# Three parts of a fused attention and feed-forward kernel redone: the value product of the first blocks, the decoding of weights, and the order of the work

## The chip, the cores and the metric

One core of a Trainium2 chip runs the whole program. Its engines are PE (TensorE, matrix products into PSUM), DVE (VectorE), ACT (ScalarE), POOL (GpSimd) and SP (SyncE, which here issues all the transfers from and to HBM and the transposes that the DMA engines make). [...] The metric is the time of the program on the device in microseconds, as the median of several runs; one execution was also taken by the profiler.

## The reference, cut to what matters

Three layers follow each other on 2304 tokens of width 512: attention with 8 heads in a window of 128 tokens, a feed-forward layer with a softmax gate and a layer norm (512 to 1024 to 512), and one with a sigmoid gate (512 to 2048 to 512).

```python
def _attn_ref(q, k, v):                      # 4 batches, 8 heads, 576 tokens, 64
    scores = scale * np.matmul(q, k.transpose(0, 1, 3, 2))
    scores = np.where(mask, scores + bias[None], -1000000000.0)
    scores = scores - np.max(scores, axis=-1, keepdims=True)
    attn = np.exp(scores)
    attn = attn / (np.sum(attn, axis=-1, keepdims=True) + 1e-09)
    return np.matmul(attn, v)
def _moe_ref(x, w_in, w_out, g_ln):
    h = x @ w_in
    sm = np.exp(h - h_max) / (sum + 1e-09)
    solu = h * sm
    ln = (solu - mu) / np.sqrt(var + 1e-06) * g_ln
    return ln @ w_out
def _moe2_ref(x, w_in, w_out):
    h = x @ w_in
    return (h * (1.0 / (1.0 + np.exp(-h)))) @ w_out
```

The weights arrive as float64, the rest as float32. The kernel's large products are made in pairs of float16 parts (high times high, high times low, low times high), three matmuls for each product.

## The kernel before, in words

The tokens are cut into 18 blocks of 128. For each block the kernel does attention (`a_qk`, `a_max` and what follows), the first feed-forward layer (`m1_in`, `layer_norm`), and for each pair of blocks, a chunk of 256 tokens, `m1_out` and then the second layer in eight steps (`m2_in`, `m2_out`).

**Weights.** Four matrices fill 48 slots of 512 float32 columns of one large tile `W`: w_in in slots 0 to 7, w_out in 8 to 15, w2_in in 16 to 31, w2_out in 32 to 47. `load_weight` (L452) takes two slots at a time: two loads of 512 KB into one `stage` buffer, of which there are two (`N_STAGE`). `decode` (L421) makes float32 of the two words of each float64: ACT works on the high words (L435), DVE casts the low words (L437) and puts the two together (L439), each over 1024 columns, both slots at once. Then the squares of each slot are summed for a scale (L473 to L489), and `split_weight` (L498) makes the two float16 parts. In `split_weight` a letter of `E_W` and of `PICK` gives each slot's operations to DVE, ACT or POOL.

**Attention of the first four blocks** (`ON_PE["a"]` is T). `a_qk` (L637) makes the scores in the bank pair `SA`, and `a_max` (L659) takes each query's maximum on DVE (L674). `t_parts` (L718) cuts the maxima into three bfloat16 parts (L729 to L732, on POOL in blocks 1 to 3) and turns them on PE (L735, copied at L738). `t_scores` (L742) makes the scores a second time, with keys on the partitions (L759, L765), and subtracts the maxima by a product (L781), so that ACT's exponents (L788) already stand as the value product needs them. `t_av` (L791) then has the values as stationary operand (128 keys x 64) and the exponents as moving one (128 keys x 128 queries); the result stands feature by feature, heads j = 0 and 1 in the two halves of the partitions. The sum of the exponents is made with a block of ones as stationary operand (L809), after a small constant is put there (L806), so that every feature's row holds the same sums.

```python
T.matmul(SA[j * HALF:(j + 1) * HALF, 0, at:at + P], vr[sl][:, 2 * p + j, :],
         a[:, j, c * P:(c + 1) * P], start=(c == 0), stop=(c == nh - 1))
...
T.matmul(SA[j * HALF:(j + 1) * HALF, 1, at:at + P], ones32.tile, a[:, j, c * P:(c + 1) * P],
         start=False, stop=(c == nh - 1))
```

`t_evac` (L813) takes for each half of the heads the reciprocal of 256 columns of sums (L824), multiplies (L827), and writes the two float16 parts (L340, L353) directly into `xT`, the turned operand of `m1_in`. A float32 product is two records in the profile.

**Attention of the other blocks.** The exponents stand query by query, are cut into float16 parts, turned by a DMA transpose (L714) and multiplied with split values (L851). `a_evac` (L856) divides, and x is then turned either on PE (`turned_parts`, L543, with the transposes of L552 and one copy and one subtraction of 512 columns, L554 and L555) or by a DMA transpose that SP issues (L879), as `ON_PE["x"]` says. The letters of that for blocks 0 to 3 are D, D, P, P, and before the change they are not used, since `t_evac` does the turning.

**The order.** Every operation is given to a list planner (`Sched`). An operation's priority is `RANK[kind] + SLOPE[kind] * i` plus an entry of `LATER` for its block; `solve` (L181) plays the engines through with modelled durations and emits each engine's instructions in the order in which they started in that model. Each engine, and SP's queue of transfers too, then works through its own list strictly in order. Pools (`Pool`) hold buffers; one with `after=` opens when the named one is closed.

Of the kernel before, what the change touches and what calls it, by code (L numbers as in the profile page):

```python
# [17 lines left out]
P = 128  # L18
# [37 lines left out]
class Op:  # L56
    __slots__ = ("turn", "buf", "alts", "eng", "cost", "fn", "prio", "succ", "n_dep", "ready", "start", "end", "idx", "dma", "done")

    def __init__(self, alts, prio, idx, dma=0):
# [9 lines left out]
        ("G", "G"): 100}  # L69


class Sched:
# [108 lines left out]
    def solve(self):  # L181
# [4 lines left out]
        todo = [o for o in self.ops if o.n_dep == 0]  # L186

# [28 lines left out]
        while n_left:  # L216
# [37 lines left out]
            t = max(free[o.eng], o.ready, port if held else 0)  # L254
            o.done, o.start = True, t
# [43 lines left out]
def fused_kernel(ctx, tc, qk, qn, kn, vt, rel, w_in, w_out, g_ln, w2_in, w2_out, out):  # L299
# [6 lines left out]
    early = Pool("early", side="right")  # L306

# [3 lines left out]
    pools = [const, early, ps, ps_early, ps_late]  # L311
# [17 lines left out]
    def act(n, fn, r=(), w=(), extra=0):  # L329
        s.op([("A", ca(n, extra), fn, False)], r, w)  # L330
# [46 lines left out]
    ones32 = Buf(early, [P, HALF], F32, "ones32")  # L377
    small = Buf(early, [P, P], BF16, "small")
# [42 lines left out]
    def decode(st, slots, at):  # L421

        def flat(x):
            return x.rearrange("p a c -> p (a c)")

        def out():
            return W.tile.bitcast(U32)[:, slots[0]:slots[1] + 1:slots[1] - slots[0], :]

        def high():
            return st[:, :, :, 1]  # L430
        w = [(W, sl) for sl in slots]
        both = [(st, 0), (st, 1)]
        if DECODE[at // 2] == "A":

            act(1024, lambda: A.activation(flat(high().bitcast(F32)), flat(high().bitcast(F32)), AF.Prelu,  # L435
                                           scale=2.0 ** 16, alpha=-2.0 ** 32), both, [(st, "high")])
            v(1024, lambda: V.tensor_scalar(flat(st[:, :, :, 0]), flat(st[:, :, :, 0]), 2.0 ** -29, 7.0, ALU.mult,  # L437
                                            ALU.min), both, [(st, "low")], fast=True)
            v(1050, lambda: V.scalar_tensor_tensor(out=out(), in0=high(), scalar=3, in1=st[:, :, :, 0],  # L439
                                                   op0=ALU.logical_shift_left, op1=ALU.bitwise_or),  # L440
              [(st, "low"), (st, "high")], w)
            return
        v(1050, lambda: V.tensor_scalar(out(), high(), 3, 0x3FFFFFFF, ALU.logical_shift_left,
                                        ALU.bitwise_and), both, w)
        v(1050, lambda: V.scalar_tensor_tensor(out=out(), in0=high(), scalar=0xC0000000, in1=out(),
                                               op0=ALU.bitwise_and, op1=ALU.bitwise_or), both + w, w)
        v(1050, lambda: V.scalar_tensor_tensor(out=out(), in0=st[:, :, :, 0], scalar=29, in1=out(),
                                               op0=ALU.logical_shift_right, op1=ALU.bitwise_or), both + w, w)
# [3 lines left out]
    def load_weight(name, w, slot0, n, cols, gain=None, columns=False, by_rows=False):  # L452
# [263 lines left out]
    x16, xT, mxs, turned_max, sts = {}, {}, {}, {}, {}  # L716

    def t_parts(i):  # L718
# [8 lines left out]
        def small_op(fn, r, w):  # L727
            s.op([("V", 85, lambda: fn(V), False), ("G", 200, lambda: fn(G), False)], r, w, pick=("tp", i))
# [62 lines left out]
    def t_av(i, p):  # L791
# [19 lines left out]
        pe(300 + 430 * nh, go, [a, ones, ones32, small] + list(vr.values()), [(SA, ("x", p % 2)), (SA, ("x", 2 + p % 2))])  # L811

    def t_evac(i, g):  # L813

        s.at("tevac", i, 10 * g)
        if g == 0:
            xT[i] = Buf(const, [P, 2, KD, P], F16, "xT", N_XT)
        t = xT[i]
        xm = Buf(const, [P, 2, 2, P], F32, "xm", 1)
        x, r = (lambda: xm[:, 0]), (lambda: xm[:, 1])  # L820

        def area(j):
            return SA[:, j, 2 * P:].rearrange("p (a t) -> p a t", t=P)
        v(256, lambda: V.reciprocal(r(), area(1)), [(SA, ("x", 2)), (SA, ("x", 3))], [(xm, 1)])  # L824
        b, z = i * P // S, (i * P + P - 1) // S
        for n, (y, lo, hi) in enumerate([(b, 0, P)] if b == z else [(b, 0, HALF), (z, HALF, P)]):
            v(2 * (hi - lo), lambda y=y, lo=lo, hi=hi: V.scalar_tensor_tensor(  # L827
                out=x()[:, :, lo:hi], in0=area(0)[:, :, lo:hi], scalar=v_scale[y].tile, in1=r()[:, :, lo:hi],
                op0=ALU.mult, op1=ALU.mult), [(SA, ("x", 0)), (SA, ("x", 1)), (xm, 1), v_scale[y]], [(xm, (0, lo))])
        xs = [(xm, (0, lo)) for lo in ((0,) if b == z else (0, HALF))]  # L830
        copy(("xh", i), 256, lambda: t[:, 0, 2 * g:2 * g + 2, :], x, xs, [(t, (0, g))])
        combine(("xl", i), 256, ALU.subtract, lambda: t[:, 1, 2 * g:2 * g + 2, :], x,
                lambda: t[:, 0, 2 * g:2 * g + 2, :], xs + [(t, (0, g))], [(t, (1, g))])
# [22 lines left out]
    def a_evac(i):  # L856
# [10 lines left out]
          [(SA, ("x", p)) for p in range(4)] + [r], [xm])  # L867
        if ON_PE["x"][i] == "P":
# [144 lines left out]
    def m2_in(c, j):  # L1013
# [16 lines left out]
        g = gp[c, j] = Buf(const, [P, 2, 2, TB], F16, "g", N_G)  # L1030
# [41 lines left out]
    s.op([("G", 250, lambda: G.memset(ones32.tile, 1.0), False)], [], [ones32])  # L1072
    s.op([("G", 350, lambda: G.memset(mparts.tile, 0.0), False)], [], [mparts])
    s.op([("G", 250, lambda: G.memset(small.tile, 0.0), False)], [], [small])
    eps = []
    for row in (0, 32, 64):
        rest = np.float32(1e-9) - np.float32(sum(eps))
        eps.append(np.float32(np.uint32(np.float32(rest).view(np.uint32) & 0xFFFF0000).view(np.float32)))
        s.op([("G", 150, lambda row=row, val=float(eps[-1]): G.memset(small[row:row + 1, :], val), False)], [], [small])
# [56 lines left out]
    for c in range(NB // 2 + 1):  # L1136
# [20 lines left out]
RANK = {"aturn": 7557.0, "av": 1601.5, "evac": -1523.1, "exp": 4766.2, "gate": -1551.3, "in": -1067.1, "in2": -263.2,  # L1157
        "load": -3596.7, "lparts": -774.7, "max": 93.3, "max1": 527.0, "norm": -7739.4, "out": -1862.5,
        "out2": 1886.9, "parts": -1408.5, "qk": 1366.1, "s0": 81.8, "s16": 807.4, "s32": 459.9, "s8": 3154.1,
        "share": -670.5, "store": 2132.5, "table": -5031.6, "tav": 99.9, "tevac": 376.2, "texp": 668.6,  # L1160
        "tpar": 2261.5, "tscore": -107.3, "tsub": 382.3, "vload": 815.2, "vnorm": -753.3, "vsplit": 444.8,
        "w0": 1558.8, "w16": 8.5, "w32": 987.0, "w8": -39.6, "xturn": -1082.2, "y": 120.5}
SLOPE = {"aturn": 55.5, "av": -16.8, "evac": 7.64, "exp": 19.41, "gate": -4.84, "in": 30.11, "in2": 1.55,
# [152 lines left out]
```

## Time and profile before

| | |
|---|---|
| median of 3 runs | 764.21 us (764.07 to 764.75) |
| the profiled execution | 760.28 us, its span 758.5 us |
| mean granted clock of PE | 0.962 |
| matmul records on PE | 5670, busy 703.5 us |

The span runs from the first to the last instruction. The profiled execution's own time is 1.8 us longer than its span, and the median of the runs is 3.9 us above the profiled execution. Busy time of PE is modelled and overlaps, so it doesn't say how close PE is to its peak. "Idle before" is the time that the engine stood still just before an instruction, and the arrow names what ended it.

### The profile page before, as it was taken

What the parts mean: (1) busy time and instruction counts of PE and PEld (TensorE: products, weight loads), DVE (VectorE), ACT (ScalarE), POOL (GpSimd) and SP (SyncE); (2) the same over time, 40 slices, a digit from 0 to 9 for tenths busy, and PEclk for the clock granted to TensorE, in tenths of its full rate; (3) what the DMA queues carried; (4) which work ended last, traced back from release to release, by engine and by line L of the source; (5) the groups of instructions that cost most, each with busy time, mean ns of one, the idle gap of its engine ahead of it and who ended that gap; (6) DMA issues with size and microseconds to landing.
All of it is one profiled execution on the core that took longest, in us unless ns stands there. A gap on an engine that the chain in (4) does not pass through costs nothing.

```text
span 758.5 us, 14323 instructions
## 1 busy us (share of the span) xinstructions
PE 703.5 (93%) x5670; PEld 478.3 (63%) x5670; DVE 458.2 (60%) x1204; ACT 357.7 (47%) x735; POOL 130.4 (17%) x126
## 2 busy tenths in 40 slices
PE   4576678999999999999999999999999999999998
PEld 3452444777765557867665777775547668757853
DVE  2569998799795685744457466466895472222220
ACT  4247665799563443644444446354562242222231
POOL 1113415342331021010021302032201010100000
PEclk9785788899999999999999999999999999999999
DMA  9265664179502475444073455154651400400000
GB/s 317 96 208 199 236 191 153 32 187 264 117 30 46 83 150 98 99 111 80 18 166 72 85 102 135 44 129 65 115 117 22 84 15 23 49 28 2 1 29 28
DMA packets 128131, 76.37 MB, mean 101 GB/s; under 512 B 110016, under 2 KB 110656, under 8 KB 128064
## 3 DMA queue, kind: packets, MB, share of 16 engines
q1 hardware_dynamic: 128064, 75.46, 41.0%
q8 instruction: 44, 0.72, 0.4%
q14 instruction: 23, 0.19, 0.1%
HBM read 44.24 MB, written 4.72 MB: 65 GB/s over the span
## 4 chain that ended last, share of the span: by engine, by line
PE 79%; DVE 11%; ACT 5%; DMA 2%; issue 2%; POOL 0%; SPq 0%; DVEq 0%; ACTq 0%; POOLq 0%
PE mm L1052 23%; PE mm L1025 22%; PE mm L893 11%; PE mm L988 11%; PE sa L647 6%; PE sa L851 2%; DVE W L439 2%; DVE xm L824 2%; DMA aT<-a 1%; PE st L765 1%; PE sa L803 1%; DVE sa L674 1%; DVE stage L437 1%; PE sa L809 1%; ACT stage L435 1%
## 5 line engine op out<-in xcount | busy, mean ns | idle before, releaser
L1025 PE MATMUL mm<-y,W 128*128 128x256 f16 x1728 | 207.0, 273 | 1.1 <-DVE t L1035 0.7
L1052 PE MATMUL mm<-W,g 128*128 128x512 f16 x864 | 205.3, 379 | 0.0
L1025 PEld LDWEIGHTS <-W 128*128 128x128 f16 x1728 | 166.6, 98 | 38.4 <-issue 1.4
L1052 PEld LDWEIGHTS <-g 128*128 128x128 f16 x864 | 81.3, 98 | 79.4 <-issue 0.6
L893 PE MATMUL mm<-W,xT 128*128 128x512 f16 x432 | 105.4, 392 | 4.7 <-POOL W L353 3.3
L988 PE MATMUL mm<-lnT,W 128*128 128x256 f16 x864 | 102.7, 273 | 0.7 <-DMA lnT<-ln 0.3
L988 PEld LDWEIGHTS <-W 128*128 128x128 f16 x864 | 83.8, 98 | 18.5 <-issue 1.8
L1034 ACT ACTIVATE t<-mm,cs 128x512 f32<-128x512 f32 x72 | 48.1, 680 | 82.7 <-PE mm L1025 82.7
L1038 DVE SCALAR_TENSOR_TENSOR g<-t,g 128x512 f16<-128x512 f32 x72 | 53.1, 741 | 52.9 <-ACT g L1037 52.5
L1035 DVE SCALAR_TENSOR_TENSOR t<-t,mm 128x512 f32<-128x512 f32 x72 | 48.8, 682 | 52.9 <-ACT t L1034 52.7
L687 ACT ACTIVATE e<-e,mx 128x256 f32<-128x256 f32 (+1 forms) x112 | 55.0, 492 | 50.1 <-DVE mx L682 49.8
L353 POOL TENSOR_TENSOR a<-e,a 128x512 f16<-128x512 f32 (+1 forms) x32 | 39.1, 1221 | 227.5 <-ACT a L340 116.9
L893 PEld LDWEIGHTS <-xT 128*128 128x128 f16 x432 | 43.0, 100 | 55.4 <-issue 13.3
L647 PE MATMUL sa<-k,q 64*128 64x128 f32 x544 | 55.5, 322 | 22.1 <-DVE mxs L674 10.6
L1037 ACT ACTIVATE g<-t 128x512 f16<-128x512 f32 x72 | 44.7, 625 | 64.8 <-PE mm L1052 59.0
L647 PEld LDWEIGHTS sa<-k,q 64*128 64x128 f32 x544 | 40.6, 204 | 42.9 <-DVE mxs L674 15.1
L907 DVE TENSOR_REDUCE lnst<-mm 128x1 f32<-128x1024 f32 x18 | 22.0, 1223 | 49.9 <-PE mm L893 47.1
L682 DVE CUSTOM_DVE_ANT_0 e<-sa,table 128x256 f32<-128x256 f32 (+1 forms) x112 | 43.7, 408 | 14.0 <-PE sa L647 4.8
L909 ACT ACTIVATE e<-mm,lnst,sig 128x1024 f32<-128x1024 f32 x18 | 21.5, 1197 | 38.8 <-DVE lnst L908 18.8
L353 POOL TENSOR_TENSOR W<-W 128x512 f16<-128x512 f32 x19 | 26.3, 1392 | 45.5 <-ACT W L340 26.0
L353 POOL TENSOR_TENSOR ln<-e,ln 128x1024 f16<-128x1024 f32 x9 | 20.6, 2293 | 77.7 <-DVE ln L341 38.9
L993 ACT ACTIVATE y<-mm,cs 128x512 f16<-128x512 f32 x18 | 12.1, 684 | 46.0 <-PE mm L988 34.6
(177 smaller groups left out, 791.9 us busy)
## 6 DMA issues: line engine op xcount, KB each, us to landing
stage<-in_moe_w_in_dram SPq DMA_DIRECT2D x24, 512.0 KB, 4.7
stage<-in_moe_w_out_dram SPq DMA_DIRECT2D x24, 512.0 KB, 4.6
k<-in_kn_dram SPq DMA_DIRECT2D x18, 256.0 KB, 3.0
q<-in_qn_dram SPq DMA_DIRECT2D x18, 256.0 KB, 3.2
vraw<-in_vt_dram SPq DMA_DIRECT2D x18, 256.0 KB, 3.0
out_dram<-t SPq DMA_DIRECT2D x18, 256.0 KB, 2.0
t<-in_vt_dram SPq DMA_DIRECT2D x16, 256.0 KB, 4.4
aT<-a SPq DMA_TRANSPOSE x56, 3.1
```

The source lines that it names most:

```text
L353: ("G", cg(n), lambda: G.tensor_tensor(dst(), a(), b(), op), True)], r, w, pick=pick)
L647: T.matmul(SA[:, j, sl * P:(sl + 1) * P], q[rows, p, :], k[rows, p, :], start=True, stop=sl not in blank)
L682: v(n + 20, lambda j=j: V.tensor_tensor_reduce(e[:, j, lo:lo + n], SA[:, j, lo:lo + n], table[:, 2 * p + j, o:o + n], -0.125, 3.0e38, ALU. ...
L687: act(n, lambda j=j: A.activation(e[:, j, lo:lo + n], e[:, j, lo:lo + n], AF.Exp, bias=mx[:, j:j + 1], scale=-1.0, accum_out=rs[:, 2 * p + ...
L893: T.matmul(pt[:, half * 512:(half + 1) * 512], x[:, hx, k, :], W16(2 * k + half, hw), start=(k == 0 and hx + hw == 0), stop=(k == KD - 1 a ...
L988: T.matmul(pt[:, ct % 2], W16(8 + k, hw)[:, ct * P:(ct + 1) * P], l[:, hx * KF1 + k, :], start=(k == 0 and hw + hx == 0), stop=(k == KF1 - ...
L1025: T.matmul(pt[:, mm], W16(16 + 4 * k + m // 4, hw)[:, (m % 4) * P:(m % 4 + 1) * P], y[:, hx, k, :], start=(k == 0 and hw + hx == 0), stop= ...
L1034: act(512, lambda: A.activation(t.tile, flat(pt.tile), AF.Tanh, scale=cs[:, 0:1]), [pt, (cs, 0)], [t], extra=1)
L1035: v(512, lambda: V.scalar_tensor_tensor(out=t.tile, in0=t.tile, scalar=1.0, in1=flat(pt.tile), op0=ALU.add, op1=ALU.mult), [t, pt], [t])
L1037: act(512, lambda: A.activation(flat(g[:, 0]), t.tile, AF.Copy, scale=2.0 ** -16), [t], [(g, 0)])
L1038: v(512, lambda: V.scalar_tensor_tensor(out=flat(g[:, 1]), in0=t.tile, scalar=2.0 ** -16, in1=flat(g[:, 0]), op0=ALU.mult, op1=ALU.subtrac ...
L1052: T.matmul(pt.tile, g[:, hg, mm, b * P:(b + 1) * P], W16(32 + m, hw), start=(m == 0 and hg + hw == 0), stop=(m == KF2 - 1 and hg == 1))
```

## The change

**The value product of the first four blocks.** The exponents become the stationary operand and the values the moving one, with a 65th column of ones beside the 64 of each head. So the result comes query by query, and its 65th column is the sum. `ones32`, `small` and the fills of POOL for them go; `v_load` now loads into rows of 65 and POOL writes ones into the 65th column for the blocks whose values are needed so.

```diff
-        at = 2 * P + (p % 2) * P
...
-            for c, (sl, _) in enumerate(halves):
-                for j in range(2):
-                    T.matmul(SA[j * HALF:(j + 1) * HALF, 0, at:at + P], vr[sl][:, 2 * p + j, :],
-                             a[:, j, c * P:(c + 1) * P], start=(c == 0), stop=(c == nh - 1))
             for j in range(2):
-                T.matmul(SA[j * HALF:(j + 1) * HALF, 1, at:at + P], ones[:, :HALF], small.tile, start=True, stop=False)
-            for c in range(nh):
-                for j in range(2):
-                    T.matmul(SA[j * HALF:(j + 1) * HALF, 1, at:at + P], ones32.tile, a[:, j, c * P:(c + 1) * P],
-                             start=False, stop=(c == nh - 1))
+                for c, (sl, _) in enumerate(halves):
+                    at = 2 * P + j * (D + 1)
+                    T.matmul(SA[:, p % 2, at:at + D + 1], a[:, j, c * P:(c + 1) * P], vr[sl][:, 2 * p + j, :],
+                             start=(c == 0), stop=(c == nh - 1))
```

**Its evacuation.** Three operations on four numbers per partition make the factor, one product of 256 columns applies it, and after both halves `x_turn` (the last part of `a_evac` before, now a function of its own) cuts x into its parts and turns it: by a DMA transpose for blocks 0 and 1, on PE for blocks 2 and 3.

```diff
-        v(256, lambda: V.reciprocal(r(), area(1)), [(SA, ("x", 2)), (SA, ("x", 3))], [(xm, 1)])
...
+        v(20, lambda: V.tensor_scalar(r.tile, heads65()[:, :, :, D], 1e-9, None, ALU.add), area, [r])
+        v(20, lambda: V.reciprocal(r.tile, r.tile), [r], [r])
+        v(20, lambda: V.tensor_scalar(r.tile, r.tile, sv.tile, None, ALU.mult), [r, sv], [r])
+        v(256, lambda: V.tensor_tensor(
+            xm[:, 4 * g:4 * g + 4, :].rearrange("p (a b) d -> p a b d", a=2), heads65()[:, :, :, :D],
+            r.tile.unsqueeze(3).to_broadcast([P, 2, 2, D]), ALU.mult), area + [r], [(xm, g)])
+        if g == 1:
+            x_turn(i, xm)
```

**Decode by slot.** A `stage` buffer holds one slot. Four are in the pool `early`; two more are in the pool `early2` and serve every third slot of the first 32. The `g` tiles of the second layer move into a pool `late`, which opens when `early2` is closed.

```diff
+    early2 = Pool("early2", side="right")
+    late = Pool("late", side="right", after=(early2,))
...
-            st = Buf(early, [P, 2, 512, 2], U32, "stage", N_STAGE)
...
+                more = slot0 < 32 and (at + z) % 3 == 2
+                s.at(f"w{slot0}", at, -800)
+                st = Buf(early2 if more else early, [P, 512, 2], U32, "stage", N_MORE if more else N_STAGE)
...
+            act(512, lambda: A.activation(high().bitcast(F32), high().bitcast(F32), AF.Prelu,
+                                          scale=2.0 ** 16, alpha=-2.0 ** 32), [(st, 0)], [(st, "high")])
+            v(512, lambda: V.tensor_scalar(low(), low(), 2.0 ** -29, 7.0, ALU.mult, ALU.min), [(st, 0)],
+              [(st, "low")], fast=True)
+            v(530, lambda: V.scalar_tensor_tensor(out=out(), in0=high(), scalar=3, in1=low(),
+                                                  op0=ALU.logical_shift_left, op1=ALU.bitwise_or),
+              [(st, "low"), (st, "high")], w)
```

**The parts of the maxima** are made by DVE in all four blocks.

```diff
-            s.op([("V", 85, lambda: fn(V), False), ("G", 200, lambda: fn(G), False)], r, w, pick=("tp", i))
+            v(16, lambda: fn(V), r, w)
```

**Order and letters.** The planner's model of PE now knows the two clock levels: it keeps an account of how busy the modelled PE was, and an instruction costs twice as much where that account calls the clock low. All numbers of `RANK`, `SLOPE` and `LATER` are new, and with them the letters of `E_W`, `NORM` and `PICK`; the one pair of slots that `DECODE` gave wholly to DVE (slots 44 and 45) goes to ACT and DVE like the others.

```diff
-E_W = "GGGVGGVGGVVGVVGGVGGVVGGVGVGGGGGVGVVGGGGVGGVGGGGG"
-DECODE = "AAAAAAAAAAAAAAAAAAAAAABA"
-NORM = "VAAAGAAVGGAVVAVGGV"
+E_W = "VGGVGGVGGVVGVVGGVGGVVGGVGVGGGGGVVVVGGVGVGGVGGGGG"
+DECODE = "AAAAAAAAAAAAAAAAAAAAAAAA"
+NORM = "VAAAGAVVVGAVAAGVAG"
...
-        "wl": "VGGGGVGGGGGVGGGGGGGVGVGGGGVVVGGGGGGVGGVGVVGGVVGG",
-        "sq": "VVGAAVGA........VVAGGAGAAGAAAAGA................", "vh": "AAAAAVVAVVAVVAVVAV",
+        "wl": "VVGGGGGGGGGVGGGGGVVVGVGGVGGVGVVGGGGVGGVGGVGGGGGG",
+        "sq": "AAGVGVAG........GVAGAAAAAAAAGAAG................", "vh": "AAAAAVAVVVVAAVAAAA",
...
-        "xl": "GGGGVVGGGGGVGGGVVV", "lh": "AAAAAVVVVVAAAVAVVV", "ll": "V.GGVVGVVGGGVGVVGG"}
-N_STAGE = 2
+        "xl": "GGGGGVVVGGVVGVGVGG", "lh": "AAAVAAAVVVAAAAAVVA", "ll": "V.VVGVVVGGGGVVVVVV"}
+N_STAGE = 4
+N_MORE = 2
...
-V_AT = [0, 1, 7, 6]
+V_AT = [0, 0, 6, 7]
```

## Rows read from the trace of the kernel before

**Rows 1.** The page, busy time, share of the span and instructions of each engine.
```profile
PE 703.5 (93%) x5670; PEld 478.3 (63%) x5670; DVE 458.2 (60%) x1204; ACT 357.7 (47%) x735; POOL 130.4 (17%) x126
```

**Rows 2.** Stretches: busy us of each engine (instructions), granted clock, DMA share, GB/s.
```profile
0.00:20.00 20.00, 9.05 (x63) 6.74 (x64) 5.48 (x31) 9.41 (x24) 3.64 (x21) 1.00 0.92 319
20.00:50.00 30.00, 19.99 (x205) 15.51 (x204) 17.93 (x31) 10.59 (x22) 3.33 (x7) 0.77 0.33 103
50.00:130.00 80.00, 57.92 (x411) 32.38 (x409) 75.05 (x171) 51.22 (x78) 30.00 (x28) 0.77 0.64 213
130.00:160.00 30.00, 26.20 (x218) 20.62 (x219) 23.50 (x56) 22.80 (x47) 11.96 (x10) 0.89 0.39 84
160.00:758.50 598.50, 590.38 (x4779) 403.06 (x4777) 336.24 (x918) 263.70 (x567) 81.51 (x61) 1.00 0.37 79
```

**Rows 3.** DVE's waits, 0 to 160 us: us in total, times, longest.
```profile
DVE xm L824 <- PE sa L809: 6.8, 3, 5.0
DVE sa L674 <- PE sa L809: 3.1, 2, 1.7
DVE e L682 <- PE sa L809: 2.4, 1, 2.4
```

**Rows 4.** The chain that ended last, 0 to 200 us, shares by line.
```profile
by line: PE sa L647 8.4%; PE mm L893 8.0%; issue 6.8%; DVE W L439 6.2%; DVE xm L824 6.1%; PE st L765 4.1%; PE mm L988 4.1%; PE sa L803 3.9%; DVE sa L674 3.3%; DVE stage L437 3.2%; PE sa L809 2.9%; ACT stage L435 2.7%; ACT W L340 2.3%; ACT W
```

**Rows 5.** Groups on PE: count, busy us, mean ns, idle before, releasers.
```profile
L803 PE MATMUL sa<-e,vraw 128*64 128x128 f32 x112 | 12.4, 347 | 4.1 <-DVE xm L827 1.6 <-DVE mxs L674 1.2 <-ACT e L788 0.7
L809 PE MATMUL sa<-e,ones 128*64 128x128 f32 x112 | 11.6, 331 | 0.0
L806 PE MATMUL sa<-small,ones 128*64 128x128 bf16 x32 | 4.5, 264 | 0.0
L647 PE MATMUL sa<-k,q 64*128 64x128 f32 x544 | 55.5, 322 | 22.1 <-DVE mxs L674 10.6 <-DMA q<-in_qn_dram 6.2 <-DVE lnst L911 2.1
L765 PE MATMUL st<-q,k 64*128 64x128 f32 x112 | 11.0, 346 | 0.0
L552 PE MATMUL mm<-unit,e 128*128 128x128 f32 x8 | 1.1, 280 | 0.0
L647 PEld LDWEIGHTS sa<-k,q 64*128 64x128 f32 x544 | 40.6, 204 | 42.9 <-DVE mxs L674 15.1 <-issue 13.1 <-DVE lnst L911 3.4
```

**Rows 6.** Groups on DVE, 0 to 160 us.
```profile
L824 DVE RECIPROCAL xm<-sa 128x256 f32<-128x256 f32 x8 | 14.0, 1753 | 7.2 <-PE sa L809 6.8 <-PE sa L653 0.3
L827 DVE SCALAR_TENSOR_TENSOR xm<-sa,sv,xm 128x256 f32<-128x256 f32 x8 | 3.8, 481 | 3.0 <-PE sa L653 1.6 <-PE sa L647 1.3
L439 DVE SCALAR_TENSOR_TENSOR W<-stage 128x1024 uint32<-128x1024 uint32 x18 | 23.9, 1327 | 0.8 <-ACT stage L435 0.4
L437 DVE TENSOR_SCALAR stage<-stage 128x1024 uint32<-128x1024 uint32 x18 | 13.0, 723 | 0.0
```

**Rows 7.** Groups on DVE, whole span, nearest to the new operations.
```profile
L862 DVE RECIPROCAL rinv<-rinv 128x8 f32<-128x8 f32 x14 | 2.8, 197 | 0.1
L341 DVE CAST W<-W 128x512 f16<-128x512 f32 x16 | 6.7, 419 | 0.0
L1035 DVE SCALAR_TENSOR_TENSOR t<-t,mm 128x512 f32<-128x512 f32 x72 | 48.8, 682 | 52.9 <-ACT t L1034 52.7
L352 DVE TENSOR_TENSOR W<-W 128x512 f16<-128x512 f32 x13 | 10.3, 798 | 0.4 <-ACT W L340 0.2
```

**Rows 8.** DMA issues: count, KB of one, us to landing.
```profile
vraw<-in_vt_dram SPq DMA_DIRECT2D x18, 256.0 KB, 3.0
xT<-x SPq DMA_TRANSPOSE x13, 3.1
```

**Rows 9.** Timelines of POOL and PE; waits of SP's queue.
```profile
84.09 0.67 POOL L353 TENSOR_TENSOR xT<-xm,xT 128x256 f16<-128x256 f32 x1 [1.59 <-ACT xT L340]
...
92.81 0.38 PE L893 MATMUL mm<-W,xT 128*128 128x512 f16 x1
...
SPq L714 <- DVE a L352: 12.9, 1, 12.9
```

More of the change, by code (lines that the diff above doesn't have):

```diff
@@ L186, in solve, with pass_windows, on_pe @@
         todo = [o for o in self.ops if o.n_dep == 0]
+        warm, window, busy = False, 0, 0.0
+        def pass_windows(t):
+            nonlocal warm, window, busy
+            while (window + 1) * CLOCK_WINDOW <= t:
+                warm = busy >= (0.4 if warm else 0.8) * CLOCK_WINDOW
+                busy = 0.0
+                window += 1
+        def on_pe(t, cost):
+            nonlocal warm, window, busy
+            pass_windows(t)
+            cost = cost if warm else 2 * cost
+            at = t
+            while (window + 1) * CLOCK_WINDOW <= t + cost:
+                busy += (window + 1) * CLOCK_WINDOW - max(at, window * CLOCK_WINDOW)
+                pass_windows((window + 1) * CLOCK_WINDOW)
+            busy += t + cost - max(at, window * CLOCK_WINDOW)
+            return cost
         def settle(o):
@@ L254, in solve @@
             t = max(free[o.eng], o.ready, port if held else 0)
+            if o.eng == "PE":
+                o.cost = on_pe(t, o.cost)
             o.done, o.start = True, t
@@ L418, in norm_scale, with decode, low @@
         return big, scl
-    def decode(st, slots, at):
-        def flat(x):
-            return x.rearrange("p a c -> p (a c)")
+    def decode(st, slot, j):
         def out():
-            return W.tile.bitcast(U32)[:, slots[0]:slots[1] + 1:slots[1] - slots[0], :]
+            return W.tile.bitcast(U32)[:, slot, :]
         def high():
[L430 to L440, printed above, removed]
+            return st[:, :, 1]
+        def low():
+            return st[:, :, 0]
+        w = [(W, slot)]
+        if DECODE[j // 2] == "A":
+            act(512, lambda: A.activation(high().bitcast(F32), high().bitcast(F32), AF.Prelu,
[4 more added lines that the diff above has]
+                                                  op0=ALU.logical_shift_left, op1=ALU.bitwise_or),
@@ L1156 @@
 PITCH = 3.3
[L1157 to L1162, printed above, removed]
@@ new lines @@
+RANK = {"aturn": 6764.2, "av": 2419.6, "evac": -2213.3, "exp": 5951.5, "gate": -2851.3, "in": -716.2, "in2": 2076.2,
+        "load": -2523.2, "lparts": -690.7, "max": -1048.4, "max1": 430.9, "norm": -7397.1, "out": -2465.8,
+        "out2": 2297.8, "parts": 105.2, "qk": 1898.3, "s0": -213.3, "s16": 821.8, "s32": 3062.6, "s8": 3384.9,
+        "share": -1654.0, "store": -227.0, "table": -7969.2, "tav": -89.5, "tevac": -186.1, "texp": 74.2,
+        "tpar": 3395.8, "tscore": -2304.5, "tsub": 361.8, "vload": 1435.2, "vnorm": -636.6, "vsplit": 854.9,
+        "w0": 2165.8, "w16": -534.7, "w32": 1448.3, "w8": 58.4, "xturn": -1294.1, "y": -2164.4}
@@ new lines @@
+SLOPE = {"aturn": 78.25, "av": -20.08, "evac": -5.04, "exp": 30.08, "gate": 10.26, "in": 14.57, "in2": -1.18,
+         "load": 23.57, "lparts": 38.24, "max": -21.52, "max1": 3.14, "norm": -13.85, "out": 0.15, "out2": 31.55,
+         "parts": 17.24, "qk": 31.07, "s0": 21.07, "s16": 1.06, "s32": 2.46, "s8": 24.89, "share": -3.61,
+         "store": -19.27, "table": 13.26, "tav": 21.68, "tevac": 19.4, "texp": 19.38, "tpar": 14.23, "tscore": 9.89,
+         "tsub": -0.61, "vload": 7.71, "vnorm": 18.06, "vsplit": 39.96, "w0": 3.34, "w16": 3.76, "w32": 3.21,
+         "w8": -4.99, "xturn": 37.39, "y": -5.59}
```

172 lines of the change are left out of this document (76 added, 96 removed), and 40 rows, old and new, of the table LATER.

## The prediction

> **What bounds the kernel now.** I read the totals first [rows 1]: PE is busy for 703.5 us of a span of 758.5, DVE for 60%. A share over the whole span hides two different stages, so the stretches come next [rows 2]. From 160 us to the end PE is busy 590.4 of 598.5 us: there only matmul work counts, and the change takes no matmul out of that stage. Before 160 us PE is busy 9.1 + 20.0 + 57.9 + 26.2 = 113.2 us and so stands still for 46.8 us of the program's 55.0. This is the ramp: the weights are decoded and split while the first four blocks of attention run. In its middle, from 50 to 130 us, DVE is busy 75.05 of 80 us, so DVE is the bound there. From 20 to 50 us no engine is full: DVE 17.9 and PE 20.0 of 30 us. That is a chain in which the two wait for each other. Over the 160 us DVE is busy 122.0 us and idle 38.0.
>
> What DVE waits for is in its waits [rows 3]: 6.8 + 3.1 + 2.4 = 12.3 us end with L809, the last matmuls of `t_av`. The chain of waits says the same from the other side [rows 4]: of its first 200 us the reciprocal of L824 holds 6.1%, 12.2 us, and L803 and L809 hold 3.9 and 2.9%, 13.6 us. These are the lines that the change removes. So the question is how much earlier the ramp ends; what follows is PE's work, which is the same.
>
> **The change, part by part.** The sum is made against the profiled execution, 760.28 us around a span of 758.5; the runs' median is 764.21, so 3.9 us are added at the end.
>
> *t_av.* L803, L806 and L809 take 12.4 + 4.5 + 11.6 = 28.5 us of PE [rows 5] in 16 calls. They go, and 112 records come that load 128 columns of exponents and stream 65 columns of values. Nothing in the trace has that shape. The upper bound is the f32 transposes of L552, which load and stream the full 128 columns: 1.1 us for 8, 140 ns each, 15.7 us in all. The lower bound is L809's own 104 ns by columns streamed, 65/128, so 53 ns and 5.9 us. Nearest are the scores L647 and L765: also two f32 records per product with 128 stationary columns, 102 and 98 ns each. They stream twice the columns but use half the rows, two at a time. I take 85 ns, a little under them: 9.5 us, a third of before. Of DVE's 12.3 us of waits on these matmuls I let two thirds go, **8.2 us**; at the upper bound of 15.7 it would be 45%, 5.5 us, at the lower 9.7.
> [...]
>
> *t_evac.* Eight reciprocals of 1753 ns and eight products of 481 ns go from DVE [rows 6], 17.9 us. In their place stand, eight times, three operations on four numbers per partition, for which L862 with 197 ns is the nearest [rows 7], and a product of 256 columns, taken at the same 481: 8 x (0.59 + 0.48) = 8.6 us. Blocks 2 and 3 now turn x on PE and pay one subtraction of 512 columns on DVE each, 0.68 us as in L1035 [rows 7], and eight transposes at 140 ns on PE, 1.1 us. DVE's net is 17.9 - 8.6 - 1.4 = **-7.9 us**.
>
> *Decode by slot.* A pair now costs two casts of 512 columns and two combinations of 512 in place of L437's 723 and L439's 1327 ns [rows 6]. By 0.42 (L341) and 0.68 (L1035) [rows 7] that is 2.20 against 2.05 us, and for the 18 pairs in the ramp **+2.7 us** of DVE. ACT also has twice the instructions, and it has room: 51 of 80 us busy [rows 2]. The one pair that DVE decoded alone lies after 160 us, where PE hides it. What the edit brings is that work can start on half a pair, and that six slots are in flight instead of four.
>
> *The parts of the maxima* (L729 to L732) go wholly to DVE: 3 blocks x 4 x 0.2 us, as L862 [rows 7], = **+2.4 us**. In return, three of four blocks lose the hop to POOL and back ahead of L735.
>
> *The letters and the order.* In the first 32 slots DVE gets six more operations of 512 columns, between 0.42 (L341) and 0.80 us (L352) each [rows 7], about 3.6 us; it loses two squares at 0.80, -1.6 us; the remainder of block 2's layer norm, 1024 columns, moves to it from POOL, twice 0.80 us. Together **+3.6 us**. After 160 us the same letters change too, and there DVE has 336 of 598 us busy [rows 2]; I put 0 and bound it by 2 us either way. Of the new order I take no gain and no loss for itself; its bounds are in the rivals.
>
> *Small things.* Five fills of POOL at the start go and four come, at about 0.2 us on an engine that is 37% busy in the ramp's middle. The loads of v are written in rows of 64 out of 65 columns, in more pieces; they take 3.0 us to land [rows 8], and 2 us more would be hidden behind the steps that make the exponents, in every block. The g tiles must wait until the two extra buffers are closed, that is until w2_in is decoded; their first writer needs that anyway.
>
> *PE's clock* was 0.77 on average between 20 and 130 us [rows 2], a mix of the two levels. [...] I count 0, as DVE and not PE is full in that stage; if PE's remaining 59 us of work there had an average of 0.70, it would cost 6 us.
>
> **Sum.** DVE's work in the ramp changes by -7.9 + 2.7 + 2.4 + 3.6 = +0.8 us, next to nothing, and its idle time falls by 8.2 us. That leaves 7.4 us; with a little for the lost hops I call it 8, give or take 6, by which the ramp ends earlier. 760.28 - 8 + 3.9 = **756 us**.
>
> **Rivals.**
> *Everything on the chain counts.* If the freed steps are refilled at once, because decode can begin sooner (DVE is idle for 12.1 of the 30 us from 20 to 50), then the gain is that of the chain: 12.2 us of L824 and 13.6 of `t_av`, less the 4.7 (eight times 0.59) and 4.5 (a third of 13.6) that replace them, about 17 us: 747 us. For it speaks that DVE's idle time is large enough; against it that DVE is full from 50 us on and gets no lighter.
> *DVE is the bound, and nothing moves.* The waits on L809 only change their name, and the 0.8 us of work comes on top: 765 us, within 0.2%. For it: 75.05 of 80 us. Against: from 20 to 50 us DVE is not full.
> *Loads of exponents bind.* The new records have no partner in another half of the array, so each could wait for its own load: L647's loads of 128 f32 columns show 204 ns each [rows 5], and 112 of them would be 22.8 us. A fifth of the 12.3 us goes, 2.5, and 0.8 of work comes: 762.5 us, just over 0.2% and counted with the same. Against it, L647's 102 ns per record hold load and stream together. [...]
> *Slower: SP's queue is held by the new transposes of x.* Before, `t_evac` left the first four blocks already turned. Now x of blocks 0 and 1 is copied, subtracted and turned by SP, with 3.1 us to landing [rows 8]. Block 1's last part was written at 84.8 us and first read at 92.8 [rows 9]; the 8 us of slack leave 4.9 for a copy and a subtraction of 512 columns, so the latency itself is hidden. But SP issues in order: a transpose at its head that waits for x holds the weight loads behind it, as one `aT` transpose waited 12.9 us [rows 9]. Six slots in flight feed DVE for 6 x 1.1 = 6.6 us; what is waited beyond that starves decode. It decides when x comes over 6.6 us after its transpose reaches SP's head. Twice 12.9 - 6.6 = 6.3 us on top of the 756 are 769 us.
>
> **How the numbers follow.** Forecast 0.54 (its own range 750 to 761), chain 0.22, bound on DVE 0.07, loads bind 0.05, SP held 0.12. A measurement of this kernel tells 0.2%, 1.5 us, from no change. Faster takes the forecast and the chain, 0.76; the same takes the bound on DVE and the loads that bind, 0.12; slower is SP held, 0.12. The range reaches to 746 and 765: beyond it lie SP held and about a third of the chain case.
>
> **What would show it.** Right: `t_av` near 9.5 us on PE; the evacuations near 1.1 us each on DVE; waits on `t_av` down to some 4 us; PE's idle time of the first 160 us smaller by about what the run gains plus what PE no longer does; the rest of the span unchanged within 2 us. The chain case shows DVE idle for under 5 us from 20 to 50 us, with decode in the gaps. Loads that bind show the new records above 200 ns apart. SP held shows `stage` waits of ACT or DVE over 6 us that end with a load queued behind an `xT` transpose. I am wrong if the gain comes after 160 us, or if the ramp shortens with DVE's idle time unchanged.

## The result, and the profile after

The changed kernel takes 755.24 us, median of 4 runs (751.62 to 756.01), against 764.14 us (762.93 to 764.75) for the kernel before beside it: a ratio of 0.9876, 95% interval 0.9842 to 0.9911. That is 7 to 12 us faster: clear of no change, and under 2%. Runs of one kernel differ with the clock that PE was granted, given as a share of the full one: the changed kernel took 751.62 us at a mean of 0.970 and 756.01 at 0.961. The profiled execution after took 756.01 us (span 754.2), the longest of its four runs. The one before took 760.28, less than all four runs beside the change. So the two pages differ by 4.3 us where the medians differ by 8.9. The pages serve here for the place of a gain, the medians for its size.

The totals after, then the stretches (us from the start, length, busy us and instructions of PE, PEld, DVE, ACT and POOL, granted clock, DMA share, GB/s), to be read beside [rows 1, 2]:

```profile
PE 705.4 (94%) x5534; PEld 481.3 (64%) x5534; DVE 460.6 (61%) x1291; ACT 363.0 (48%) x754; POOL 101.9 (14%) x97
```

```profile
0.00:20.00 20.00, 9.92 (x64) 7.36 (x65) 6.87 (x38) 10.25 (x25) 2.94 (x19) 1.00 0.91 250
20.00:50.00 30.00, 21.30 (x147) 15.66 (x147) 24.37 (x71) 17.55 (x36) 5.48 (x6) 0.84 0.89 307
50.00:130.00 80.00, 61.05 (x370) 38.74 (x368) 73.13 (x206) 58.13 (x106) 20.13 (x15) 0.74 0.64 197
130.00:160.00 30.00, 26.87 (x241) 20.96 (x239) 27.72 (x73) 21.56 (x46) 7.48 (x6) 0.89 0.59 143
160.00:754.20 594.20, 586.28 (x4720) 398.61 (x4718) 328.55 (x908) 255.52 (x544) 65.85 (x51) 1.00 0.34 72
```

Read the last stretch first. PE still stands idle for 594.20 - 586.28 = 7.9 us of it, as it did for 8.1 before. What has shrunk is the work that is left at 160 us: 586.3 us of PE instead of 590.4, 4.1 us less, nearly all of the 4.3 by which the two pages differ. So what the pages show of the gain was made in the ramp. PE stands still there for 40.9 of the 160 us (46.8 before). DVE is busy for 6.87 + 24.37 + 73.13 + 27.72 = 132.1 of the 160 us (122.0 before) and idle for 27.9 (38.0 before). Most of that change is in one stretch, 20 to 50 us: 24.4 us busy instead of 17.9. The kernel does more of its decode in the same 160 us, 44 slots instead of 18 pairs. It does not come to the end of its first four blocks sooner. The last call of `t_av` before, and the line with the last two calls after (start, us, what), end at 137.76 and at 142.85 us:

```profile
136.67 1.09 PE L809 MATMUL sa<-e,ones 128*64 128x128 f32 x8
...
140.81 2.04 PE L830 MATMUL sa<-vraw,e 128*128 128x65 f32 x16 [1.78 <-DVE xm L848]
```

What the new order makes of the time is other work of the ramp, done earlier.

DVE's waits of the first 160 us (us in total, times, longest), to be read beside [rows 3]. The first line is of the kernel before, the others are of the changed one:

```profile
DVE sa L674 <- PE sa L647: 10.4, 8, 3.6
...
DVE sa L701 <- PE sa L674: 9.3, 7, 3.1
...
DVE W L462 <- ACT stage L458: 2.4, 3, 1.2
DVE xm L848 <- PE sa L674: 2.3, 1, 2.3
DVE rinv L845 <- PE sa L674: 2.2, 1, 2.2
...
DVE rinv L845 <- PE sa L830: 0.7, 1, 0.7
```

In the changed kernel L830 is the new `t_av`, L674 the scores, L701 the maxima, and L845 to L848 the evacuation. The 12.3 us of waits on L809 have become 0.7 us on L830. The waits of the maxima on the scores are still there: 9.3 us, where they were 10.4 before. A wait is put down to the matmul that ended last, so a name alone can mislead: the evacuation also waits 2.3 + 2.2 = 4.5 us for the scores now, where it waited 3.2 for them before. All its waits on PE together were 10.0 us before and are 5.2 now, and all of DVE's waits on matmuls into `sa` fell from 26.3 to 16.0 us.

The groups that answer to [rows 5] on PE, and to [rows 6] on DVE from 0 to 160 us (count, busy us, mean ns, idle before):

```profile
L830 PE MATMUL sa<-vraw,e 128*128 128x65 f32 x112 | 17.4, 316 | 4.8 <-DVE xm L848 4.8
```

```profile
L845 DVE TENSOR_SCALAR rinv<-sa 128x4 f32<-128x4 f32 x8 | 1.2, 152 | 2.9 <-PE sa L674 2.2 <-PE sa L830 0.7
L846 DVE RECIPROCAL rinv<-rinv 128x4 f32<-128x4 f32 x8 | 1.4, 170 | 0.1
L847 DVE TENSOR_SCALAR rinv<-rinv,sv 128x4 f32<-128x4 f32 x8 | 3.5, 433 | 0.0
L848 DVE TENSOR_TENSOR xm<-sa,rinv 128x256 f32<-128x256 f32 x8 | 3.3, 417 | 2.4 <-PE sa L674 2.3
L462 DVE SCALAR_TENSOR_TENSOR W<-stage 128x512 uint32<-128x512 uint32 x44 | 32.2, 737 | 3.3 <-ACT stage L458 2.4 <-ACT sq L502 0.5
L460 DVE TENSOR_SCALAR stage<-stage 128x512 uint32<-128x512 uint32 x45 | 21.0, 470 | 0.1
```

The evacuations cost DVE 1.2 + 1.4 + 3.5 + 3.3 = 9.4 us in place of 17.9. A pair of slots costs it 2 x (0.737 + 0.470) = 2.41 us in place of 2.05. And PE's value product shows 17.4 us, far from the 9.5 of the prediction.

How much shorter is it, then? Here a group's busy time misleads. Two calls of the old `t_av` on PE's timeline (start, us, what), one short and one long:

```profile
40.40 1.12 PE L803 MATMUL sa<-e,vraw 128*64 128x128 f32 x8
41.31 0.32 PE L806 MATMUL sa<-small,ones 128*64 128x128 bf16 x2
41.41 1.07 PE L809 MATMUL sa<-e,ones 128*64 128x128 f32 x8
...
44.11 0.66 PE L803 MATMUL sa<-e,vraw 128*64 128x128 f32 x8
44.60 0.23 PE L806 MATMUL sa<-small,ones 128*64 128x128 bf16 x2
44.66 0.61 PE L809 MATMUL sa<-e,ones 128*64 128x128 f32 x8
```

The lines overlap: L806 starts 0.49 us after L803, not 0.66. From first start to last end the second call takes 45.27 - 44.11 = 1.16 us, where its three rows add to 1.50; the first takes 2.08. And lines of the new product, with the clock of the stretches around the first and the last (columns as above). These calls have 8 records each, so a line of x16 is two calls:

```profile
40.34 2.00 PE L830 MATMUL sa<-vraw,e 128*128 128x65 f32 x16
...
85.93 1.02 PE L830 MATMUL sa<-vraw,e 128*128 128x65 f32 x8
...
98.01 3.47 PE L830 MATMUL sa<-vraw,e 128*128 128x65 f32 x16 [1.31 <-DVE xm L848]
```

```profile
40.00:46.00 6.00, 4.30 (x42) 3.71 (x40) 5.78 (x15) 3.95 (x9) 1.09 (x1) 0.98 0.83 268
...
98.00:101.50 3.50, 3.49 (x17) 3.43 (x18) 2.79 (x9) 1.54 (x3) 0.00 (x0) 0.53 0.31 83
```

In windows of 1 us from 20 to 160 us the granted clock reads 1.00 or 0.50 in both kernels, apart from the windows in which it changes. Around the first line it is 0.98, and 16 records take 2.00 us, 125 ns each by the length of the whole line; around the last it is 0.53, and they take 3.47 us, 217 ns each. So a call of 8 records takes 1.02 us where the old one took 1.16, both at a granted clock of 1.00 (the old call of 2.08 us stood at 0.50). Added up over all calls in that way, the old `t_av` held PE for 21.5 us and the new one holds it for 17.4: 4.1 us less, not the 11.1 that the groups' sums show.

### The profile page after: what moved, and what is told of

It reads as the page before. It is cut to its first block, busy times and chain, and to the rows that moved or that the text cites. A ratio compares the mean times of both kernels' runs of the same rounds, so it can differ in the third digit from the quotient of the medians.

```text
span 754.2 us, 14101 instructions
## 1 busy us (share of the span) xinstructions
PE 705.4 (94%) x5534; PEld 481.3 (64%) x5534; DVE 460.6 (61%) x1291; ACT 363.0 (48%) x754; POOL 101.9 (14%) x97
## 4 chain that ended last, share of the span: by engine, by line
PE 69%; DVE 4%; DMA 3%; ACT 1%; issue 1%; SPq 0%; DVEq 0%; ACTq 0%
PE mm L1076 23%; PE mm L1049 20%; PE mm L1012 11%; PE mm L917 9%; PE sa L674 4%; PE sa L870 2%; DMA aT<-a 1%; DVE e L709 1%; DMA k<-in_kn_dram 1%; DMA lnT<-ln 1%; DVE xm L883 0%; DVE a L378 0%; DVE ln L378 0%; DVE t L1059 0%; ACT g L1061 0%
## 5 line engine op out<-in xcount | busy, mean ns | idle before, releaser
L1049 PE MATMUL mm<-y,W 128*128 128x256 f16 x1728 | 211.0, 274 | 0.0
L917 PE MATMUL mm<-W,xT 128*128 128x512 f16 x432 | 102.5, 390 | 6.9 <-ACT mm L942 6.0
L1062 DVE SCALAR_TENSOR_TENSOR g<-t,g 128x512 f16<-128x512 f32 x72 | 51.0, 709 | 77.6 <-ACT g L1061 77.4
L917 PEld LDWEIGHTS <-xT 128*128 128x128 f16 x432 | 42.3, 100 | 60.0 <-issue 15.5
L674 PE MATMUL sa<-k,q 64*128 64x128 f32 x544 | 54.5, 318 | 16.3 <-DMA q<-in_qn_dram 5.5
L379 POOL TENSOR_TENSOR a<-e,a 128x512 f16<-128x512 f32 (+1 forms) x29 | 35.2, 1216 | 201.9 <-ACT a L366 132.0
L674 PEld LDWEIGHTS sa<-k,q 64*128 64x128 f32 x544 | 39.9, 201 | 34.5 <-issue 12.6
L462 DVE SCALAR_TENSOR_TENSOR W<-stage 128x512 uint32<-128x512 uint32 x48 | 35.8, 750 | 3.3 <-ACT stage L458 2.4
L1020 DVE SCALAR_TENSOR_TENSOR y<-mm,cs,y 128x512 f16<-128x512 f32 x18 | 13.1, 747 | 36.5 <-ACT y L1017 36.4
L458 ACT ACTIVATE stage<-stage 128x512 f32<-128x512 f32 x48 | 31.2, 663 | 2.1 <-DMA stage<-in_moe_w_in_dram 2.1
```

The costliest lines, as they stand in the source:

```text
L462: v(530, lambda: V.scalar_tensor_tensor(out=out(), in0=high(), scalar=3, in1=low(), op0=ALU.logical_shift_left, op1=ALU.bitwise_or), [(st, ...
L674: T.matmul(SA[:, j, sl * P:(sl + 1) * P], q[rows, p, :], k[rows, p, :], start=True, stop=sl not in blank)
L917: T.matmul(pt[:, half * 512:(half + 1) * 512], x[:, hx, k, :], W16(2 * k + half, hw), start=(k == 0 and hx + hw == 0), stop=(k == KD - 1 a ...
L1049: T.matmul(pt[:, mm], W16(16 + 4 * k + m // 4, hw)[:, (m % 4) * P:(m % 4 + 1) * P], y[:, hx, k, :], start=(k == 0 and hw + hx == 0), stop= ...
L1062: v(512, lambda: V.scalar_tensor_tensor(out=flat(g[:, 1]), in0=t.tile, scalar=2.0 ** -16, in1=flat(g[:, 0]), op0=ALU.mult, op1=ALU.subtrac ...
```

## The experiments

Theories. **A**, the prediction's: DVE's time and idle time in the ramp set when it ends; PE's own time counts only through DVE's waits. **B**: the new order, planned with another model of PE, gains by itself. **C**: PE's shorter value product is the gain. **D**, formed after the runs with every instruction in its place: DVE and PE stand in one chain in the ramp, and what is taken from either counts nearly in full.

### Parts of the change in orders made for other work

Four kernels shared their chip's runs of the kernel before (762.32 us). e1 has only the new value product, evacuation, turn of x and load of v; e2 only decode by slot with its six buffers; e3 all the new operations in the old planner's order; e4 the old operations in the new one's. None has numbers of its own for its order.

```
e1_value      + xm[:, 4*g:4*g+4, :] <- heads65()[..., :D] * r      (hunks of t_av, t_evac, x_turn, v_load)
e2_decode     + decode(st, slots[z], slot0 + at + z)               (hunks of decode, pools, N_STAGE, N_MORE)
e3_old_order  + every hunk of the work    - pass_windows, new RANK, SLOPE, LATER, letters
e4_new_order  + pass_windows, new RANK, SLOPE, LATER, letters      - every hunk of the work
```

> The kernel before with the new value product, its evacuation and the turns of x alone; old decode, old planner, old numbers and letters. Theory A (DVE's time and idle time in the ramp set its end; the reciprocals are worth about 8 us of DVE, the matmuls themselves little, since the new records take 111 ns each at the full clock): about 760 us, 3 to 5 less than before. Theory B (the new order is what gains; a part under numbers that were not made for it gains nothing): 763 to 767. Theory C (PE's time in the value product gains): 756 or less.

> The kernel before with decode by slot and six buffers alone; old value product, old planner, old numbers and letters. Theory A: decode fills DVE's gaps before 50 us, but costs some 0.18 us more per slot, so 760 to 763. Theory B: 764 to 768, since the extra work of decode is paid and the order doesn't use the buffers. Theory C: 764, no change.

> The changed kernel with the old planner, the old numbers and the old letters: all the edits of the work, none of the order. Theory A: 756 to 760, most of the gain. Theory B: 763 to 768, no gain. Theory C: 755 to 757, all of it.

> The kernel before with the new planner, its new numbers and letters alone; old value product and old decode in pairs. Theory A: 762 to 765, since DVE has as much to do as before and its waits on the sums stay. Theory B: 755 to 758. Theory C: 764.

Measured: e1 762.23 us, 1.0010 (0.9983 to 1.0036); e2 776.32, 1.0200 (1.0177 to 1.0222); e3 790.61, 1.0381 (1.0346 to 1.0415); e4 772.93, 1.0155 (1.0140 to 1.0170). Only e1 fits a theory: its ratio, taken of the 764.14 us before, is 765 us, and B expected 763 to 767. The other three lie outside all that was expected. All four are slower than the whole change, and all work edits together in the old order lose 3.8%. What follows is only that order and work are fitted to each other. Numbers made for one set of operations cost up to 3.8% on another, which hides any part's own worth, so these runs don't decide between A, B and C.

### The same order, one cost taken away or put back

To leave the order out of it, four kernels keep every instruction in its place and change what one of them costs. Three stand on the kernel before (763.04 us beside them): p3 copies where L824 took the reciprocal, so x is not divided; p4 leaves out L809, the 56 products (112 records) with `ones32`, so the row sums are a constant from `small`; p5 does both. p1 stands on the changed kernel and gives DVE a reciprocal of 252 columns, whose result nobody reads, ahead of each evacuation.

```diff
 p3, p5
-        v(256, lambda: V.reciprocal(r(), area(1)), ...
+        v(256, lambda: V.tensor_copy(r(), area(1)), ...
 p4, p5
-                T.matmul(SA[...], ones[:, :HALF], small.tile, start=True, stop=False)
-            for c in range(nh):
-                ...
+                T.matmul(SA[...], ones[:, :HALF], small.tile, start=True, stop=True)
 p1
+        V.reciprocal(SA[:, :, 2 * P + 2 * (D + 1):], SA[:, :, 2 * P:4 * P - 2 * (D + 1)])
```

> The kernel before, every instruction in its old place, with a copy of the 256 sums on DVE in place of their reciprocal (x is then not divided): 8 x some 1.3 us less of DVE. Theory A (DVE's time in the ramp sets its end): 4 to 8 less than the kernel before. Theory B (the gain is in the order, which is unchanged here): within 1.5. Theory C (PE's time in the value product): within 1.5.

> The kernel before, every instruction in its old place, without the products that sum the exponents (L809); a constant stands for the sums. 11.6 us less of PE in the ramp. Theory A: 0 to 3 less than the kernel before, by DVE's waits on L809. Theory B: within 1.5. Theory C: 8 to 11 less.

> Both at once: the kernel before in its old order without the sums' products and with copies for the reciprocals; x is neither divided nor scaled by its sums. Theory A: 6 to 11 less than the kernel before, little more than without the reciprocals alone. Theory B: within 2. Theory C: 8 to 11 less, the same as without the sums alone.

> The changed kernel, every instruction in its place, with a reciprocal of 252 columns put back on DVE ahead of each evacuation's first operation (its result is not used): 8 x some 1.75 us more of DVE. Theory A: 7 to 14 more than the changed kernel's 755.2, so 762 to 769: the gain is gone. Theory B: 755 to 758. Theory C: 755 to 757.

The evacuation's group of p3, and then of p1, which show what was taken and given (columns as above):

```profile
L824 DVE COPY xm<-sa 128x256 f32<-128x256 f32 x8 | 3.4, 420 | 6.9 <-PE sa L809 6.3 <-PE sa L653 0.3 <-PE sa L647 0.2
```

```profile
L846 DVE RECIPROCAL sa<-sa 128x252 f32<-128x252 f32 x8 | 13.9, 1732 | 2.8 <-PE sa L674 2.8
```

| | taken or given | median | ratio (95%) | us of time | per us |
|---|---|---|---|---|---|
| p3 | DVE -10.6 (14.0 to 3.4) | 751.41 | 0.9842 (0.9811 to 0.9874) | -12.1 | 1.14 |
| p4 | PE -8.2 (21.5 to 13.3, first start to last end) | 755.60 | 0.9891 (0.9865 to 0.9917) | -8.3 | 1.0 |
| p5 | both | 746.86 | 0.9782 (0.9750 to 0.9815) | -16.6 | 0.9 |
| p1 | DVE +13.9 | 766.31 | 1.0045 (1.0025 to 1.0065) | +12.9 against the change | 0.93 |

The last column is the price: us of run time for each us taken or given. (p1's 12.9 us are (1.0045 - 0.9876) x 763.04; with both intervals, give or take 3. By the same intervals each price is uncertain by 0.2 to 0.3.) Of the ranges expected, p1's met A's. p3 and p5 gained more than any theory allowed; p4's 8.3 us are above A's 0 to 3 and within C's 8 to 11, while C had p3 within 1.5.

Look at p3's idle time ahead of L824: DVE still waits 6.3 us there for L809 (6.8 in the kernel before), and yet the run is 12.1 us shorter. A wait that stays did not eat the gain: what comes after DVE comes earlier. In p3's trace the last two calls of `t_av` start at 121.74 and 123.56 us, 12.1 us earlier than in the kernel before (133.87 and 135.71). That speaks for A's first half. p4 speaks against its second: 8.2 us of PE were worth 8.3, while DVE's waits on matmuls into `sa` fell only from 26.3 to 24.3 us. A DVE that is busy for 75 of 80 us from 50 to 130 us doesn't make PE's time free. The reason offered is that in each block the scores, DVE's maxima, the exponents, the value product and the evacuation follow one another. That is D.

Two things keep these prices rough. The single profiled runs give lower ones: 0.90 for p3 and 0.83 for p1, but 0.60 for p4, whose last two calls of `t_av` start only 2.1 and 3.0 us earlier. So DVE's price near 1 stands by both, while PE's lies anywhere from about a half to 1. And the granted clock was not held fixed: over the first 160 us its mean is 0.82 before and after the change, but 0.88 in p3 and 0.84 in p4 and p1, so part of p3's gain may be the clock's.

p1 shows that DVE's price still holds in the changed kernel: it gives DVE back 13.9 us, more than the 8.5 that the evacuation lost, and more than the whole gain goes.

### Parts of the change, each with an order made for it

Last, the planner's numbers and letters were searched again for each set of operations, all from the old numbers and in the same way. r0 has the old operations and the new planner; r1 adds the new value product and keeps the decode in pairs; r2 adds decode by slot and keeps the old value product. p2 stands on the changed kernel and multiplies each value product a second time, into columns that nobody reads. The kernel before took 763.35 us beside them.

```diff
 r0: + class Sched of the change, numbers searched for the old operations
 r1: r0 + t_av, t_evac, x_turn, v_load of the change, numbers searched for these
 r2: r0 + decode, early2, late of the change, numbers searched for these
 p2
+                    T.matmul(SA[:, p % 2, at + 61 * j:at + 61 * (j + 1)], a[:, j, c * P:(c + 1) * P],
+                             vr[sl][:, 2 * p + j, :61], start=(c == 0), stop=(c == nh - 1))
```

> The kernel before with no edit of its work: only the planner's new model of PE, and its numbers and letters searched again from the old ones. Theory B (order alone is the gain): 753 to 757. Theory D (DVE and PE stand in one chain in the ramp; what is taken from either counts nearly in full, and the value product is the part that takes): 758 to 764.

> The same search with the new value product, evacuation and turns of x, but the old decode in pairs and four slots in flight. Theory D: 748 to 756, as good as the changed kernel or better, since decode by slot costs DVE and is not what gains. Decode as the gain: 759 to 764. Theory B: 753 to 757, as with the order alone.

> The same search with decode by slot and six buffers, but the old value product. Theory D: 760 to 767. Decode as the gain: 753 to 757. Theory B: 753 to 757.

> The changed kernel, every instruction in its place, with each value product made a second time into columns that nobody reads: 112 more records, some 12 to 17 us of PE. Theory A (only DVE's time counts in the ramp): 755 to 758. Theory C and theory D: 763 to 769.

Measured: r0 765.77 us, 1.0027 (1.0004 to 1.0050); r1 753.74, 0.9903 (0.9869 to 0.9936); r2 770.14, 1.0108 (1.0074 to 1.0142); p2 761.98, 0.9999 (0.9963 to 1.0034). The value product's group on PE and decode on DVE, 0 to 160 us, in r1, then decode in r2 and in r0:

```profile
L828 PE MATMUL sa<-vraw,e 128*128 128x65 f32 x112 | 18.3, 322 | 2.5 <-ACT e L813 2.0 <-DVE xm L846 0.5
L461 DVE SCALAR_TENSOR_TENSOR W<-stage 128x1024 uint32<-128x1024 uint32 x20 | 27.2, 1361 | 5.8 <-ACT stage L457 5.6
```

```profile
L464 DVE SCALAR_TENSOR_TENSOR W<-stage 128x512 uint32<-128x512 uint32 x42 | 34.9, 839 | 1.2 <-DVE xT L367 0.3
L463 DVE SCALAR_TENSOR_TENSOR W<-stage 128x1024 uint32<-128x1024 uint32 x22 | 28.4, 1291 | 3.6 <-ACT stage L459 3.3
```

r0 gains nothing: B falls, as far as this search goes. r1 has the whole gain within its interval, so the new value product with its evacuation is the part that takes. r2 loses 8 us: with the old value product decode by slot only costs, and its row says what (839 ns for half of what took r0 1291 ns). D's ranges held r1; r0 and r2 came out 2 and 3 us above theirs. In p2 the two sets of products hold PE for 30.2 us instead of 17.4 and the run is (0.9999 - 0.9876) x 763.35 = 9.4 us longer than the change, give or take 3.7, that is 0.73 per us of PE (0.64 if one run of 769.98 us is left out, 7 us above the next of the eight, and 0.52 by the single profiled runs), and nothing of the gain is left. So PE's time is not free. But DVE's waits on matmuls into `sa` grow by 8.2 us in p2, from 16.0 to 24.2, so p2 alone doesn't tell D from A's second half, by which PE counts through DVE's waits.

## Why the prediction was right, and where not

**Time, sign and place: right.** 756.0 was forecast and 755.24 measured. As forecast, PE's idle time after 160 us stayed (7.9 us, 8.1 before), and DVE's idle time in the ramp fell: by 10.1 us for the 8.2 named. The clock, counted at 0, stayed: from 20 to 130 us (30 x 0.84 + 80 x 0.74) / 110 = 0.77, as before. One sign was set up wrongly: work that PE no longer does in the ramp adds to its idle time there, so the idle time could not shrink by the gain plus that work. It shrank by 6.0 us.

**The terms, however, were off in both directions, and the sum came out by their cancelling.**

- *`t_av` at 9.5 us*: 17.4, outside its own bounds of 5.9 to 15.7. The nearest rows, L647's 102 ns, were products that load and stream only half the rows, 64 of 128, two at a time: at 51.80 us two records of 272 ns stand within 0.28 us. Their loads show 204 ns each in [rows 5], so that 102 ns "hold load and stream together" was a misreading. The new record has 128 rows and took 125 ns at a granted clock of 0.98, 217 at 0.53; how much of that is its load was not shown. The upper bound of 140 ns was taken at the higher clock alone (1.00 at L552), for a stage whose mean clock stood in [rows 2] at 0.77.
- *28.5 us of old `t_av`*: these were three groups' busy times with overlapping records. From first start to last end it was 21.5, so PE's saving is 4.1 us and not the 19 of the text.
- *"PE counts only through DVE's waits", two thirds of 12.3 us*: 11.6 went by name, and 10.3 of all of DVE's waits on matmuls into `sa`, though the calls got only a fifth shorter. p4 gained 8.3 us where DVE's waits on matmuls fell by 2.0, so PE's time also counts in another way. Nor did the waits go only because PE is faster. In the trace, DVE now decodes between them: its work on W from 20 to 50 us is 12.8 us instead of 6.0.
- *Evacuation -9.3 before the turns of x*: -8.5, right. The three small operations were taken at 197 ns each; two took 152 and 170, L847 433 (below).
- *Decode +0.15 us per pair*: +0.36. *Maxima +2.4 us*: L756 to L759 hold DVE for 0.6 + 1.4 + 1.6 + 1.7 = 5.3 us in four blocks, where DVE spent 0.7 on its one block before: +4.6.
- *DVE's work in the ramp +0.8 us*: 132.1 - 122.0 = +10.1. But 160 us is a mark in time and not in work, and eight more slots at 1.21 us are decoded by then, 9.7 us. The comparison of the two stretches was the wrong one to forecast; the one to make is the same work at its old and its new price.

With the measured prices the sum is: evacuation 8.5 us of DVE at 0.93 to 1.14, and 4.1 us of PE at 0.73 to 1.0, 11 to 14 us gross. r1 against r0, which differ by this, the turns of x and the numbers searched for each, shows (1.0027 - 0.9903) x 763.35 = 9.5 us, give or take 3.1. The change as a whole shows 8.9, though it also pays for the dearer decode (18 x 0.36 = 6.5 us of DVE) and the maxima (4.6). So the sum by prices does not close for the whole change: something in it gives back about as much as those cost.

**The rivals.** *Everything on the chain counts* came nearest to the mechanism: p3, p5 and p1 show it for DVE's time, p4 for PE's, there with a rough price. DVE is idle for 5.6 us from 20 to 50 us, just above the 5 that it named, with decode in the gaps as it said. It failed by its size: 17 us supposed that `t_av` shrinks to a third, and nothing for dearer decode. *DVE is the bound and nothing moves* falls with p4 and the result. *Loads of exponents bind* had the record's size (over 200 ns) only at the low clock (217 ns at 0.53), and its 762.5 us is far above the 755.24 measured. *SP's queue held* did not show. The transposes it named, from SP's timeline, wait 1.7 us at most (`SPq L903 <- PE mm L917: 1.7, 1, 1.7`):

```profile
36.12 1.35 SPq L903 DMA_TRANSPOSE xT<-x  x1
...
62.52 1.27 SPq L903 DMA_TRANSPOSE xT<-x  x1
```

The longest wait for a load of weights in the ramp is ACT's, from that trace's waits: `ACT stage L458 <- DMA stage<-in_moe_w_in_dram: 2.1, 2, 1.7`, 1.7 us where this rival needed over 6.

**Left open.** The worth of decode by slot inside the whole change: r1 without it and the change overlap (0.9903 and 0.9876), while r2 shows it costing 8 us beside the old value product. That it pays by its earlier start and larger number of buffers, and so closes the sum above, is argued and not shown; the new order could do it as well. The search behind r0 to r2 was limited, and a longer one could move each of them by some us. The maxima on DVE and the turns of x were not tried alone, and no run held the granted clock fixed.

## What to carry to other kernels

Where two engines hand work back and forth, price both: take an operation's time away with every instruction left in its place, and see what the run gives back per us. Quote each price with its interval. For a call whose lines overlap on PE, take first start to last end and not the sum of its groups, and price a new matmul at each level of clock that its stage shows (here 125 ns at 0.98 and 217 at 0.53). Don't judge a part of a change in an order planned for something else: here kernels in such orders lost up to 3.8%.

## What the hardware showed that was not expected

Two of L847's eight operations on DVE, each on four numbers per partition, lasted until an operation of POOL beside them ended: 0.94 and 1.19 us, where the other six took 0.22 to 0.23. The timeline of both engines at 96 us, then L847's durations (min/median/max ns, first and last start):

```profile
95.91 1.21 POOL L503 TENSOR_TENSOR sq<-W 128x512 bf16<-128x512 f32 x1 [4.66 <-PE mm L513]
...
96.20 0.94 DVE L847 TENSOR_SCALAR rinv<-rinv,sv 128x4 f32<-128x4 f32 x1
```

```profile
L847 DVE TENSOR_SCALAR rinv<-rinv,sv x8: 216/224/1185, 23.6 to 146.5; 128x4 f32<-128x4 f32 x8
```

L847's median is 224 ns, but here it takes 940 ns and ends within 0.02 us of POOL's square; its slowest takes 1185, from 138.64 us, and ends within 0.03 us of POOL's L379 (138.63, 1.17 us). Two such cases of eight make L847's mean 433 ns. L757 and L758 do the same once each, at 32 and 33 us: they take 0.95 and 1.08 us on 8 columns and end 0.02 and 0.03 us after an operation of POOL. What holds them so long was not shown. L847 is better priced by its mean of 433 ns than by its median of 224.

A reciprocal of 256 f32 columns from PSUM cost DVE 1753 ns [rows 6] where the copy of the same columns in p3 took 420, four times as much; on 4 columns it took 170.
